# An SSD layer and a four-branch expert layer on one TensorE: the opening in another order, weight sums in pairs, one block of scores two products sooner

## The chip, the cores and the metric

One core of a Trainium2 chip runs the whole program in one launch. The core has TensorE (PE, matrix products; its weight loads are shown apart as PEld), VectorE (DVE), ScalarE (ACT), GpSimd (POOL) and SyncE (SP, which here issues almost all transfers). The metric is the device time of one launch in microseconds, as the median of several runs; lower is better. A separate execution is recorded by the profiler; the lines below come from it.

## The reference

The first part is a chunked state-space layer (32 pairs of batch and head, 768 steps, head width 32, state width 16). The second multiplies its output, 3072 tokens of 256 channels, with four experts and adds them, weighted by the normalised `domain_probs`. In brief (`la` is the logarithm of `a` in the chunk):

```python
    for c in range(nc):
        cum = np.cumsum(la, axis=-1)
        L = np.exp(cum[:, :, :, None] - cum[:, :, None, :]) * causal
        M = np.einsum('bhin,bhjn->bhij', Cc, Bc) * L
        y_intra = np.einsum('bhij,bhjd->bhid', M, xc)
        y_inter = np.einsum('bhin,bhnd->bhid', Cc, state) * np.exp(cum)[..., None]
        y[:, :, sl] = y_intra + y_inter
        state = decay_full * state + np.sum(Bx, axis=2)
...
    p = domain_probs / (domain_probs.sum(-1, keepdims=True) + 1e-09)
    for e in range(E):
        h = np.maximum(x @ w1[e], 0.0)
        out += p[:, e:e + 1] * (h @ w2[e])
```

## The kernel before

Everything is float32. The sequences are cut in chunks of 128 steps, 24 in all (4 batches by 6), numbered so that chunk `c` belongs to batch `c % 4`. A chunk holds all 8 heads, as 4 quarters of two. For each chunk the kernel makes *scores* (`score`, L502: C times B), *decays*, their product `MT` (`masked`, L681, or L856 in the plan), and from it with the values `xb` the chunk's output and its state (`inner`, L546; for later chunks also L879, which adds the state carried over). Decays of the first three chunks come from the raw `a`: `spread` (L660) copies a row to all partitions by a matmul with ones, and `scan` (L519) multiplies along it; chunks 3 to 5 scan a copy `ab` that was loaded with every row on all partitions (from `acut_d`, which the kernel writes itself); later ones use an exponential of sums of logarithms (`cum_d`).

The expert part is done as a fast matrix multiplication: 20 products instead of 24 for three pairs of chunks (a block) and four slices of weights of 256 hidden units (a unit; scheme `G`), and 7 instead of 8 for the first of them (scheme `B`). It needs sums of weights: `G.sums` lists them, `operands` makes them (L1024, one sum of 128x256 after another, on GpSimd or VectorE), stores them to `w_d` for the next block, and loads them again later. Two sums share a tile of 128x512 (`G.shared`). Four of the eight raw blocks are needed as they are (`G.raw`); where the sums are read back, these are loaded half a tile at a time (128 KB). A product is `product` (L933), two matmuls of 128x128 by 128x256, each of which shows as two records; `gated` (L968) applies the ReLU and the weight of the expert, `combine` (L960), `adjust` (L1071), `snap` (L942) and `seed` (L947) form the sums on the other side, `outputs` copies the output of a chunk (L894) and its state (L556).

Two ways of ordering the work stand beside each other. The opening, down to the first product, is written out by hand: loads on SyncE, preparation on GpSimd and VectorE (`clip`, L608; `pc`, L619, the normalised probabilities), then `spread`, `score`, `scan_quarters`, `aside` (ScalarE copies a score tile out of PSUM, L675, and GpSimd multiplies it, L676), `masked` (VectorE multiplies out of PSUM, L681), `fade` (L540, the part of the state), `turn_gates` (L646, a transpose and its copy `p_sb`, L647), `spread_gate` (L652) and `inner`. `idle` (L684) issues matmuls whose result nobody reads. The rest goes through a planner (`Plan`): each piece of work has a duration per engine, values it reads and writes, and the planner fixes the order of every engine's instructions by simulated times, from a start `now` and a time at which each engine is free (`plan.run`). The order in TensorE's line is given (`line`); `PAIRS_AT` says at which product of which unit the scores (`s`) and the outputs (`o`) of a pair of chunks stand. Each engine's queue is fixed in the program: an instruction that waits holds up what stands behind it, on SyncE and ScalarE also transfers.

Of the kernel before, what the change touches and what calls it, by code (L numbers as in the profile page):

```python
# [31 lines left out]
URGENT = {}  # L32
# [6 lines left out]
HORIZON, OPENING, LOADED = 26.0, 80.0, 1.0  # L39
ORDERS = (0, 1, 2, 3), (3, 1, 2, 0), (0, 1, 2, 3), (3, 1, 2, 0)  # L40
PAIRS_AT = ((1, 24, "s0"), (2, 1, "o0"), (2, 1, "s1"), (2, 24, "s2"), (3, 1, "o12")), (
# [28 lines left out]
class Plan:  # L70
# [109 lines left out]
    def run(self, line, at, begin):  # L180
# [17 lines left out]
        self.stall, self.port, self.bus = [], 0.0, begin["SP"] + 4  # L198
# [103 lines left out]
class Scheme:  # L302
# [9 lines left out]
G.sums = ((15, 13, 10, -1), (9, 11, 10, -1), (0, "a", 16, -1), (2, "c", 11, -1), (1, "c", 13, -1),  # L312
          (14, 16, 13, -1), (3, "e", 10, -1), (7, 10, "c", -1), (18, "d", 10, -1), (17, "d", 16, -1),
          (8, 16, 11, -1), (19, "a", 13, -1), (6, "a", 11, -1), (12, 13, "d", -1), (5, "e", 16, -1),
          (4, 11, "e", -1))
# [6 lines left out]
G.shared = {1: ((15, 9), (0, 2), (1, 14), (3, 7), (18, 17), (8, 19), (5, 6), (12, 4)),  # L322
            2: ((9, 15), (7, 2), (19, 3), (17, 12), (14, 4), (8, 5), (18, 1), (6, 0))}
# [36 lines left out]
def kernel(  # L360
# [60 lines left out]
    def some(n, shape, name, pool=const):  # L421
# [19 lines left out]
        "dram": [None],  # L441
# [137 lines left out]
    nc.sync.dma_start(out=xb[0][:, OBT:], in_=xbc[real(0)][:, OBT:])  # L579
    nc.sync.dma_start(  # L580
        out=a_sb, in_=a.rearrange("c h s -> (c h) s").rearrange("(p r) s -> p r s", r=2))
    nc.sync.dma_start(out=xb[1][:, OBT:], in_=xbc[real(1)][:, OBT:])
# [4 lines left out]
    load_tokens(2, xb[2])  # L587

# [18 lines left out]
    def clip(engine, v, top=1.0):  # L607
# [11 lines left out]
    nc.gpsimd.tensor_mul(  # L619
        pc.rearrange("p (k q) e -> p q k e", q=NSEQ), pr.rearrange("p (q k) e -> p q k e", q=NSEQ),  # L620
        total_p.rearrange("p (q k) e -> p q k e", q=NSEQ).to_broadcast([P, NSEQ, NC, E]))
# [5 lines left out]
    nc.gpsimd.memset(a_cut[:, :, 0:1], 0.0)  # L627

# [3 lines left out]

    store_decays(nc.sync, acut_d, a_cut)
    load_tokens(3, xb[3])
    for fb in range(2, 4):
        load_w1(fb, homes["W"][fb])
    for fb in range(4):
        load_w2(fb, homes["W"][4 + fb])
    load_decays(3, homes["ab"][0])
# [31 lines left out]
    gs = [homes["W"][-1][:, NT * P * i:NT * P * (i + 1)].rearrange("p (t s) -> p t s", t=NT) for i in range(2)]  # L671
# [21 lines left out]
    idle(BANK[7], 3)  # L693
    spread(0, four)
    idle(BANK[6], 3)
    mask(0, ctm[0], xb[0])
    score([0], ctm[:1], xb[:1], seven)
    scan_quarters(0, LT[0], four, 0)
    aside(0, 0, seven[0])
    aside(0, 1, seven[1])  # L700
# [288 lines left out]
    def operands(k, scheme, fbs, l, loaded={}, keep=True):  # L989
# [8 lines left out]
        def view(r):  # L998
            return views[r]()
# [564 lines left out]
```

## Time and profile before

| | us |
|---|---|
| median of 3 runs | 612.3 (612.06 to 612.62) |
| the profiled execution, whole | 612.72 |
| its span, first to last instruction | 610.94 |
| first product (L933) begins | 12.61 |
| last copy of a result on ScalarE ends | 607.73 |
| TensorE busy in the span | 603.7 |

The profile has a page (busy time of each engine, 40 slices, the chain of work that ended last, groups of instructions) and can be asked for more: a timeline, tables by stage, waits. A line of the timeline has the start, the length, the engine, the line of the kernel, the operation, out and in with partitions and elements, how many instructions are merged in it, and in square brackets the idle time before it and what ended it. The page's 40 slices of 15.3 us give the busy share of each engine in tenths; GpSimd works in the first half of the span only:

```profile
DVE  7899997988879894887969988396785989575775
ACT  5267365487642327868352334734444142434441
POOL 6565546556461001676400100200000000000000
```

### The profile page before, as it was taken

What the parts mean: (1) busy time and instruction counts of PE and PEld (TensorE: products, weight loads), DVE (VectorE), ACT (ScalarE), POOL (GpSimd) and SP (SyncE); (2) the same over time, 40 slices, a digit from 0 to 9 for tenths busy, and PEclk for the clock granted to TensorE, in tenths of its full rate; (3) what the DMA queues carried; (4) which work ended last, traced back from release to release, by engine and by line L of the source; (5) the groups of instructions that cost most, each with busy time, mean ns of one, the idle gap of its engine ahead of it and who ended that gap; (6) DMA issues with size and microseconds to landing.
All of it is one profiled execution on the core that took longest, in us unless ns stands there. A gap on an engine that the chain in (4) does not pass through costs nothing.

```text
span 610.9 us, 10142 instructions
## 1 busy us (share of the span) xinstructions
PE 603.7 (99%) x3365; PEld 513.6 (84%) x3365; DVE 489.8 (80%) x854; ACT 292.9 (48%) x681; POOL 158.8 (26%) x238
## 2 busy tenths in 40 slices
PE   9999999999999999999999999999999999999997
PEld 5778778888888888888888888888888888888885
DVE  7899997988879894887969988396785989575775
ACT  5267365487642327868352334734444142434441
POOL 6565546556461001676400100200000000000000
PEclk9999999999999999999999999999999999999999
DMA  7757668566853429893332425863142232953001
GB/s 253 257 185 222 194 215 326 187 213 228 285 160 98 113 36 328 280 313 124 134 117 87 149 47 140 274 237 118 55 127 80 87 91 63 341 187 121 1 0 53
DMA packets 89060, 99.65 MB, mean 163 GB/s; under 512 B 27428, under 2 KB 58928, under 8 KB 89008
## 3 DMA queue, kind: packets, MB, share of 16 engines
q1 hardware_dynamic: 88852, 98.95, 51.3%
q8 instruction: 27, 0.44, 0.3%
q14 instruction: 25, 0.20, 0.1%
q10 hardware_dynamic: 156, 0.06, 0.0%
HBM read 78.80 MB, written 20.17 MB: 162 GB/s over the span
## 4 chain that ended last, share of the span: by engine, by line
PE 92%; DVE 2%; ACT 1%; issue 0%; DVEq 0%
PE bank L933 88%; PE bank L546 2%; PE bank L502 1%; PE bank L879 1%; ACT A L556 1%; DVE v L968 1%; DVE v L960 0%; DVE MT L856 0%; ACT v L894 0%; DVE bank L1071 0%; DVE v L1260 0%; PE bank L1325 0%; DVE v L1425 0%; ACT LT L894 0%; ACT v L1330 0%
## 5 line engine op out<-in xcount | busy, mean ns | idle before, releaser
L933 PE MATMUL bank<-v,w 128*128 128x256 f32 x1676 | 394.8, 380 | 0.8 <-DVE bank L1071 0.7
L933 PEld LDWEIGHTS bank<-v,w 128*128 128x128 f32 x1676 | 316.9, 190 | 48.2 <-issue 2.2
L933 PE MATMUL bank<-Y,w 128*128 128x256 f32 x692 | 177.6, 381 | 0.7 <-ACT LT L894 0.4
L1213 ACT COPY v<-bank 128x512 f32<-128x512 f32 x109 | 64.0, 587 | 178.5 <-PE bank L933 166.2
L933 PEld LDWEIGHTS bank<-Y,w 128*128 128x128 f32 x692 | 130.2, 190 | 22.4 <-issue 2.0
L968 DVE SCALAR_TENSOR_TENSOR v<-bank,gate 128x512 f32<-128x512 f32 x149 | 102.3, 688 | 42.6 <-PE bank L933 39.7
L960 DVE TENSOR_TENSOR v<-v,v 128x512 f32<-128x512 f32 x181 | 126.6, 719 | 1.7 <-ACT v L942 0.3
L1071 DVE TENSOR_TENSOR bank<-bank,v 128x512 f32<-128x512 f32 x84 | 57.4, 696 | 35.7 <-PE bank L933 23.4
L942 ACT COPY v<-bank 128x512 f32<-128x512 f32 x100 | 58.6, 587 | 54.0 <-PE bank L933 45.0
L1024 POOL TENSOR_TENSOR w<-w,w 128x256 f32<-128x256 f32 x94 | 73.1, 794 | 42.5 <-DVE v L960 14.5
L947 ACT COPY bank<-v 128x512 f32<-128x512 f32 x127 | 74.0, 595 | 10.7 <-DVE v L968 8.7
L933 PE MATMUL bank<-LT,w 128*128 128x256 f32 x208 | 52.7, 379 | 0.0
L526 ACT ACTIVATE MT<-ab,neg 128x128 f32<-128x128 f32 x144 | 47.1, 396 | 2.1 <-DMA ab<-cum_d 2.1
L933 PEld LDWEIGHTS bank<-LT,w 128*128 128x128 f32 x208 | 39.4, 190 | 5.3
L531 POOL TENSOR_SCALAR_AFFINE_SELECT MT<-MT 128x512 f32<-128x512 f32 x36 | 23.2, 655 | 69.2 <-ACT MT L526 53.9
L1024 POOL TENSOR_TENSOR w<-w 128x256 f32<-128x256 f32 x32 | 24.3, 763 | 18.8 <-DVE Y L1043 7.7
L960 DVE TENSOR_TENSOR v<-bank,v 128x512 f32<-128x512 f32 x26 | 17.9, 688 | 11.1 <-PE bank L933 9.9
L856 DVE TENSOR_TENSOR MT<-bank,MT 128x512 f32<-128x512 f32 x36 | 22.7, 681 | 0.1
L1260 DVE TENSOR_TENSOR v<-v,v 128x256 f32<-128x256 f32 x55 | 21.1, 422 | 1.0 <-ACT v L1213 0.7
L960 POOL TENSOR_TENSOR v<-v,v 128x512 f32<-128x512 f32 x6 | 7.7, 1277 | 49.7 <-DVE v L960 49.7
L968 DVE SCALAR_TENSOR_TENSOR v<-v,gate 128x512 f32<-128x512 f32 x26 | 19.8, 763 | 0.4
L495 ACT ACTIVATE ctm<-xb,tmask 128x128 f32<-128x128 f32 x48 | 15.8, 395 | 3.8 <-DMA xb<-in_xbc_dram 3.7
(110 smaller groups left out, 315.1 us busy)
## 6 DMA issues: line engine op xcount, KB each, us to landing
w<-w_d SPq DMA_DIRECT2D x128, 256.0 KB
w_d<-w SPq DMA_DIRECT2D x64, 256.0 KB
w<-in_w_dram SPq DMA_DIRECT2D x40, 256.0 KB
ab<-cum_d SPq DMA_DIRECT2D x18, 512.0 KB
w<-in_w_dram SPq DMA_DIRECT2D x64, 128.0 KB
gate<-p_d SPq DMA_DIRECT2D x15, 384.0 KB
xb<-in_xbc_dram SPq DMA_DIRECT2D x17, 192.0 KB
out_dram<-v SPq DMA_DIRECT2D x144, 16.0 KB
```

Of the source, the lines that this page charges most:

```text
L526: nc.scalar.activation(out=MT[:, place(c, h), 0:P], in_=ab[:, h * P:h * P + P], func=AF.Exp, bias=neg[:, h % NT, NQ * real(c) + h // NT:NQ ...
L531: nc.gpsimd.affine_select(out=MT[:, h:h + n, 0:P], in_=MT[:, h:h + n, 0:P], compare_op=ALU.is_ge, fill=0.0, base=0, pattern=[[0, n], [1, P ...
L856: nc.vector.tensor_mul(to, g, LT0[:, js, h] if cs[0] < SCANNED else to)
L933: nc.tensor.matmul(out=o, lhsT=w[:, j], rhs=x if half is None else x[:, j], start=(start and j == 0), stop=(j == 1), skip_group_check=True)
L942: act(.5, lambda e: nc.scalar.copy(out=flat(v), in_=bank.t), reads=[bank], writes=[v])
L947: act(.54 if to - lo > FB else .32, lambda e: nc.scalar.copy(out=bank.t[:, lo:to], in_=flat(v)[:, lo:to]), reads=[v], writes=[bank])
L960: plan.add(engines, lambda e: (on(e).tensor_add if sign > 0 else on(e).tensor_sub)(flat(v), whole(x), whole(y)), reads=[x, y], writes=[v], ...
L968: dve(D512, lambda e: nc.vector.scalar_tensor_tensor(out=h.t, in0=whole(x).rearrange("p (j m) -> p j m", j=JJ), scalar=0.0, in1=g.t[:, 2 * ...
L1024: plan.add(B256, lambda e, r=r, x=x, y=y, sign=sign: (on(e).tensor_add if sign > 0 else on(e).tensor_sub)(view(r), view(x), view(y)), two= ...
L1071: dve(D512, lambda e: (nc.vector.tensor_add if sign > 0 else nc.vector.tensor_sub)(to.t, bank.t, whole(x)), reads=[x, bank], writes=[to])
L1213: act(.5, lambda e: nc.scalar.copy(out=flat(v), in_=bank.t), reads=[bank], writes=[v], hold=HOLD)
L1260: plan.add(engines, lambda e: (on(e).tensor_add if sign > 0 else on(e).tensor_sub)(o[1](), x[1](), y[1]()), reads=[v for v in vs if v is n ...
```

## The change

The opening's loads: tokens of chunk 1 are issued before `a`; chunk 3's tokens and the third and fourth slice of w1 follow at once; the store of `a_cut` moves from SyncE to ScalarE's queue; chunk 3's `ab` is loaded before the four slices of w2, not after. `pc` is computed after `a` is clipped. The third `idle` goes, and the second has two tiles, not three. Both chunks' C are masked ahead of the scores. Of chunk 0, all four score tiles go by `aside` (two went by `masked`); of chunk 1, all four by `masked` (one went by `aside`). Chunk 1's spread and scans come before that; the gate's spread comes before chunk 0's output, and chunk 2's spread, which the planner placed, stands by hand before chunk 1's output. The logarithm, its sums and the stores of `cum_d` and `p_d` go to the planner, whose start, free times and some durations change. `G.sums` names pairs of sums made by one instruction of 128x512 (7 pairs and 2 single sums, where there were 16), `G.shared` pairs them so, and raw blocks are loaded in pairs as one transfer of 256 KB (`load_pair`). The scores of the second block's first pair stand at product 22 of the unit, not 24.

```diff
-HORIZON, OPENING, LOADED = 26.0, 80.0, 1.0
+HORIZON, OPENING, LOADED = 26.0, 80.0, -1.0
-PAIRS_AT = ((1, 24, "s0"), (2, 1, "o0"), (2, 1, "s1"), (2, 24, "s2"), (3, 1, "o12")), (
+PAIRS_AT = ((1, 22, "s0"), (2, 1, "o0"), (2, 1, "s1"), (2, 24, "s2"), (3, 1, "o12")), (
...
+G.ends = ("a", "c"), ("d", "e")
+G.sums = (((15, 9), (13, 11), 10), (0, "a", 16), ((1, 2), "c", (13, 11)), ((14, 8), 16, (13, 11)),
+          ((18, 3), ("d", "e"), 10), (7, 10, "c"), ((17, 5), ("d", "e"), 16),
+          ((19, 6), "a", (13, 11)), ((12, 4), (13, 11), ("d", "e")))
...
+G.shared = {1: ((15, 9), (0, 7), (1, 2), (14, 8), (18, 3), (17, 5), (19, 6), (12, 4)),
+            2: ((15, 9), (0, 7), (1, 2), (19, 6), (18, 3), (17, 5), (12, 4), (14, 8))}
...
     nc.sync.dma_start(out=xb[0][:, OBT:], in_=xbc[real(0)][:, OBT:])
+    nc.sync.dma_start(out=xb[1][:, OBT:], in_=xbc[real(1)][:, OBT:])
     nc.sync.dma_start(
         out=a_sb, in_=a.rearrange("c h s -> (c h) s").rearrange("(p r) s -> p r s", r=2))
-    nc.sync.dma_start(out=xb[1][:, OBT:], in_=xbc[real(1)][:, OBT:])
...
     load_tokens(2, xb[2])
+    load_tokens(3, xb[3])
+    for fb in range(2, 4):
+        load_w1(fb, homes["W"][fb])
...
-    store_decays(nc.sync, acut_d, a_cut)
-    load_tokens(3, xb[3])
-    for fb in range(2, 4):
-        load_w1(fb, homes["W"][fb])
-    for fb in range(4):
-        load_w2(fb, homes["W"][4 + fb])
-    load_decays(3, homes["ab"][0])
...
     idle(BANK[6])
-    idle(BANK[7], 3)
+    idle(BANK[7], 2)
     spread(0, four)
-    idle(BANK[6], 3)
     mask(0, ctm[0], xb[0])
+    mask(1, ctm[1], xb[1])
     score([0], ctm[:1], xb[:1], seven)
     scan_quarters(0, LT[0], four, 0)
     aside(0, 0, seven[0])
     aside(0, 1, seven[1])
+    store_decays(nc.scalar, acut_d, a_cut)
     scan_quarters(0, LT[0], four, 1)
-    fade(0, MT[0], xb[0], LT[0])
-    mask(1, ctm[1], xb[1])
     spread(1, four)
     for r in (2, 3):
-        masked(0, r, MT[0], LT[0], seven[r], 0)
-    turn_gates(BANK[7])
-    nc.scalar.activation(out=a_sb, in_=a_sb, func=AF.Ln)
-    next_ = [BANK[4], BANK[0], BANK[1], BANK[6]]
+        aside(0, r, seven[r])
+    fade(0, MT[0], xb[0], LT[0])
+    turn_gates(seven[0])
+    load_decays(3, homes["ab"][0])
+    for fb in range(4):
+        load_w2(fb, homes["W"][4 + fb])
+    score([1], ctm[1:], xb[1:2], seven)
     scan_quarters(1, LT[1], four, 0)
-    score([1], ctm[1:], xb[1:2], next_)
-    aside(1, 0, next_[0])
-    y = BANK[7][:, :NT * (P + N)].rearrange("p (t s) -> p t s", t=NT)
+    spread_gate(four[0], homes["gate"][0])
+    y = four[1][:, :NT * (P + N)].rearrange("p (t s) -> p t s", t=NT)
     for t in range(NT):
         inner(0, t, y[:, t], xb[0], MT[0], P + N, t == 0)
...
-    spread_gate(BANK[5], homes["gate"][0])
-    for r in (3, 1, 2):
-        masked(1, r, MT[1], LT[1], next_[r], 0)
...
-    store_decays(nc.sync, cum_d, sums)
+    for r in (3, 0, 1, 2):
+        masked(1, r, MT[1], LT[1], seven[r], 0)
+    third = [seven[0], seven[3], four[2], four[3]]
+    spread(2, third)
...
-    nc.sync.dma_start(out=p_d.rearrange("e c s -> c e s"), in_=p_sb)
...
-    now = 13.2
+    now = 12.0
...
-    def source(fb, l, i):
+    def load_pair(v, fbs, l, f, i):
 
-        e, f = divmod(fb, EPB)
+        e, fb = divmod(fbs[f], EPB)
         if l == 1:
-            return w1[e, i * P:i * P + P, f * FB:f * FB + FB]
-        return w2[e, f * FB:f * FB + FB, i * P:i * P + P].rearrange("(j p) m -> p j m", p=P)
+            nc.sync.dma_start(out=v.t, in_=w1[e, i * P:i * P + P, fb * FB:fb * FB + 2 * FB])
+        else:
+            nc.sync.dma_start(
+                out=v.t.rearrange("p (j m) -> p j m", m=P),
+                in_=w2[e, fb * FB:fb * FB + 2 * FB, i * P:i * P + P].rearrange("(j p) m -> p j m", p=P))
...
+        def both(r):
+            if r in where and isinstance(r, tuple):
+                return where[r].t.rearrange("p (a j f) -> p a j f", a=2, j=JJ)
+            return view(r).unsqueeze(1).to_broadcast([P, 2, JJ, P])
...
+            for pair in (*scheme.raw, *(() if keys[0] in w_d else scheme.ends)):
+                v = value("W")
+                paired(v, pair)
+                f, i = scheme.blocks[l][pair[0]]
+                dma(lambda e, v=v, f=f, i=i: load_pair(v, fbs, l, f, i), part=[v])
...
+            for r, x, y in scheme.sums:
+                if isinstance(r, tuple):
+                    plan.add(B512, lambda e, r=r, x=x, y=y: difference(e, both(r), both(x), both(y)),
+                             two=True, reads=[where[x], where[y]], part=[where[r]], lean=True)
...
+    act(.3, lambda e: nc.scalar.activation(out=a_sb, in_=a_sb, func=AF.Ln), writes=[logs])
+    for r in range(2):
+        dve(.35, lambda e, r=r: sum_logs(e, r), reads=[logs], part=[cum])
+    dma(lambda e: store_decays(nc.sync, cum_d, cum.t), kb=96, reads=[cum], writes=[cd])
+    dma(lambda e: nc.sync.dma_start(out=p_d.rearrange("e c s -> c e s"), in_=p_sb), kb=48, writes=[pd])
...
-    done = plan.run(line, now, {"PE": now, "DVE": now - .2, "ACT": now + 1.0, "POOL": now - 2.0,
+    done = plan.run(line, now, {"PE": now, "DVE": now - .8, "ACT": now + 1.1, "POOL": now - 1.2,
                                 "SP": now + LOADED})
```

## The prediction

> **What bounds the kernel now.** I read the share of busy time first, then the chain of work that ended last, then a table of stages, then the opening's timeline, and last the weight-load rows with an idle time before them. The page:
>
> ```profile
> PE 603.7 (99%) x3365; PEld 513.6 (84%) x3365; DVE 489.8 (80%) x854; ACT 292.9 (48%) x681; POOL 158.8 (26%) x238
> ...
> PE 92%; DVE 2%; ACT 1%; issue 0%; DVEq 0%
> ```
>
> TensorE is the bound: 92% of the chain. The stages that I cut (start:end, length, then each engine's busy time, clock, DMA share, GB/s) show how tight:
>
> ```profile
> 3.74:12.60 8.86, 8.51 (x84) 4.81 (x83) 7.92 (x19) 4.92 (x17) 5.13 (x10) 1.00 0.95 303
> 12.60:24.30 11.70, 11.70 (x70) 9.96 (x66) 9.12 (x15) 4.08 (x14) 7.80 (x13) 1.00 0.84 284
> 24.30:56.00 31.70, 31.51 (x214) 23.70 (x213) 30.22 (x50) 19.59 (x53) 17.38 (x26) 1.00 0.64 204
> 56.00:125.00 69.00, 67.75 (x466) 56.52 (x465) 61.75 (x110) 37.65 (x110) 38.84 (x58) 1.00 0.70 231
> ...
> 235.00:601.00 366.00, 366.00 (x1900) 318.35 (x1899) 280.11 (x469) 169.23 (x357) 49.90 (x67) 1.00 0.45 141
> ```
>
> From 235 us on TensorE never rests, and no product is added or taken out, so nothing can be won there. What can move is the start of the first product (L933 at 12.60) and the waits between it and 125 us, where VectorE is 95% busy (30.22 of 31.70) and then 89%. The opening, from the timeline (start, length, engine, line, what ended the idle time):
>
> ```profile
> 4.67 1.07 POOL L608 TENSOR_SCALAR cum<-cum 96x256 f32<-96x256 f32 x1
> ...
> 4.68 2.43 DVE L519 TENSOR_TENSOR_SCAN LT<-bank,ident 128x256 f32<-128x256 f32 x4 [0.17 <-PE bank L660]
> ...
> 6.62 1.42 POOL L676 TENSOR_TENSOR MT<-w,LT 128x256 f32<-128x256 f32 x2 [0.27 <-ACT w L675]
> ...
> 7.03 0.73 DVE L681 TENSOR_TENSOR MT<-bank,LT 128x256 f32<-128x256 f32 x2
> ...
> 7.68 2.42 DVE L519 TENSOR_TENSOR_SCAN LT<-bank,ident 128x256 f32<-128x256 f32 x4
> ...
> 10.82 1.21 PE L546 MATMUL bank<-MT,xb 128*32 128x144 f32 x16
> ...
> 11.96 0.71 PE L660 MATMUL bank<-v,const-float32-1.0 32*128 32x256 f32 x8
> ...
> 12.61 3.72 PE L933 MATMUL bank<-v,w 128*128 128x256 f32 x16
> ...
> 13.55 2.43 DVE L519 TENSOR_TENSOR_SCAN LT<-bank,ident 128x256 f32<-128x256 f32 x4
> ```
>
> VectorE sets the pace: two masked products (7.03) stand between the scans of chunks 0 and 1, and chunk 2's scans wait until 13.55. The waits that follow (weight-load rows):
>
> ```profile
> 25.19 0.89 PEld L546 LDWEIGHTS bank<-MT,xb 128*32 128x32 f32 x30 [0.40 <-DVE MT L856]
> ...
> 43.22 2.46 PEld L933 LDWEIGHTS bank<-Y,w 128*128 128x128 f32 x12 [0.41 <-ACT v L942]
> ...
> 47.20 0.73 PEld L933 LDWEIGHTS bank<-v,w 128*128 128x128 f32 x4 [0.47 <-DVE v L968]
> ...
> 72.94 2.46 PEld L933 LDWEIGHTS bank<-v,w 128*128 128x128 f32 x12 [1.06 <-POOL w L1024]
> ...
> 82.47 0.73 PEld L933 LDWEIGHTS bank<-Y,w 128*128 128x128 f32 x4 [0.84 <-ACT LT L894]
> ...
> 123.35 0.73 PEld L933 LDWEIGHTS bank<-Y,w 128*128 128x128 f32 x4 [0.53 <-ACT v L894]
> ```
>
> About 0.23 of such an idle time is there at every change of work. Products follow each other 0.216 us a record; beyond that I count 0.45 lost at 24-26 us, 1.3 in seven small waits from 31 to 48, 0.85 at 72 (the row names GpSimd, but VectorE's L1071 ended only at 72.82), 0.44 at 82, 0.3 at 123 and again near 232: 3.6 us in all.
>
> **The opening, step by step.** SyncE now issues tokens of chunk 1 (0.43 us) ahead of `a`, so `a` is issued at 2.8, not 2.35; the clip started 2.32 after its issue (4.67), so now at 5.1. GpSimd then runs clip, copy, memset (starts 1.14, 0.45 and 0.1 apart: to 6.8), `pc` (moved behind them, 0.4) and four masked products where there were two before the fade, 0.68 apart: 7.2, 7.9, 8.6, 9.3. Chunk 0's fade ends near 10.4 (8.41 before), chunk 1's at 10.7.
>
> ScalarE masks chunk 1 early, copies two score tiles (0.37 each, to 6.5), issues the store of `a_cut` once GpSimd's memset is done (6.9), and copies two more by 7.9. Those wait behind the store, and GpSimd needs the third at 8.6: covered by 0.9 us. On SyncE that store took 0.34; ScalarE's two issues in this trace took 0.40 and 1.19, so at worst the cover is just used up.
>
> VectorE loses the two masked products, so chunk 1's scans run 7.05 to 9.43 instead of 7.68 to 10.10, and chunk 1's masked products, now four (0.34 apart, the first 0.1 after the scan), end at 10.96, against 11.29.
>
> TensorE is as before up to chunk 1's scores (8.43, behind the 0.26 us copy of `p_sb`; 0.67 to the next). Then the gate's spread (1.1), and chunk 0's output product, free at 10.2 but waiting for the fade: 10.4. Then spread of chunk 2 at 11.03 (0.63 later, as 9.10 to 9.73), chunk 1's output at 11.67 (0.64, as 11.96 to 12.60), done 0.70 later at 12.37; ScalarE's copy (0.27) now stands bare, where chunk 2's spread covered it: first product at **12.7**, 0.1 later than before. Bounds: without the wait for GpSimd 12.5; with `a` 0.8 later still (1.19 on SyncE, and its turn behind the next load) 13.5. I take 12.7, since every term has a row. The filler matmuls taken out (0.91 at 4.59) let chunk 0's scores start 0.35 earlier, which buys nothing: the scans, not the scores, are next in line.
>
> **After the first product.** Chunk 2's spread now precedes the wait for chunk 1, so its scans start at 11.8 instead of 13.55. `ab` of chunk 3 is loaded behind the early store, ahead of the four w2 loads: its scan started at 19.22 because the DMA came then, and now waits for VectorE at about 15.9 (two sums of logs, 0.35 each, and one gate, 0.65, come first). Adding 2.34 for that scan, 0.65 for each gate and 0.6 for each of the four L856 products, these end at 22.5, against 25.14. TensorE asks for them at 12.1 after its first product, 24.8. So the 0.45 goes; bounds 0 to 0.5. The four w2 loads queue behind that wait on SyncE and land some 1.5 us later (512 KB at about 350 GB/s); the first is used 8.4 us after the first product, at 21, and landed near 14: covered.
>
> ScalarE's logarithm (0.42) and SyncE's stores of `p_d` and `cum_d` move behind the first product; the heads' decays that read `cum_d` were loaded by 22.3 and serve L879 at 33.89, so 4 us later is covered.
>
> VectorE is then 2.3 to 2.6 us ahead. Of the 1.3 us at 31-48, the waits on L968 are answers of a queue that is full and those on L942 are ScalarE's copies, which the lead doesn't shorten; bounds 0 to 1.3, I take half, 0.65.
>
> Sums two at a time: 144 of 256 columns become 32, and 56 of 512. GpSimd: 126 by 0.77 to 0.79 (97.4 us) become 30 by 0.79 and 50 by 1.28 (87.5). VectorE: 18 by 0.42 become 2 by 0.42 and 6 by 0.72, 2.4 us less, and with four fewer L960 (0.72) 5.3 less. This lies beside TensorE; it counts only as slack at 24-125 us. A paired sum reads one operand twice; no row shows that form on GpSimd, the nearest (L968, broadcast gate, VectorE) takes 0.69, less than a plain 0.72, so I price it as plain; if it took double (2.55), 64 us would be added over 200 us of an engine that is 50 to 60% busy there, and the sums would come late by some us: it widens the upper end by 1. The 64 raw loads of 128 KB become 32 of 256 KB: SyncE saves about 32 by 0.45, for which nobody waits, as DMA is 64 to 70% busy there.
>
> Scores two products sooner: after them stood two products (1.73 us), and the third waited 0.85 for L1071, queued behind a L856 and a L968. Now four products (3.47) stand there, and the adjustment follows two L856: about 3.1 after the scores' start, against a need at 4.6. I take 0.7 of the 0.85; bounds -0.3 (the scores themselves find a bank not free) to 0.85. The waits on L894 (82, 123, 232) come from ScalarE's copies, which are not touched: 0.
>
> **Sum.** +0.1 - 0.45 - 0.65 - 0.7 = -1.7. The profiled execution took 612.72 (span 610.94 and 1.78 around it), 0.4 over the median of 612.3; so 611.0 for it, and **610.6** for the median.
>
> **Rivals.**
> (1) The opening gets earlier too, which the change's constants claim (the plan's start goes from 13.2 to 12.0). For it: VectorE and the tail of chunk 1 are earlier. Against: scores at 8.43 and five TensorE steps behind them. It would need about 1.2 off, 609.4.
> (2) The lead buys nothing: small waits are latencies from TensorE through ScalarE and back, and at 72 GpSimd's sum (the name in the row) takes L1071's place. For it: L942 and L894 names, and GpSimd's half-full queue; against: VectorE at 95%. Only the 0.45 is won, 0.1 lost: 612.0.
> (3) Slower: the warm-up. The first four filler records took 3.18 us for 1,792 columns (1.77 ns each), the products 3.72 for 4,096 (0.91): TensorE starts at about half rate. Fillers are cut from 2,560 column passes to 1,536, so TensorE rests from about 3.5 to 3.95 and 4.7 to 5.05. If the full rate then comes only after chunk 1's scores, the steps from 8.43 (0.67, 1.1, 0.63, 0.64, 0.70: 3.7 us) double: 610.6 + 3.7 = 614.3. It decides from 8.4 us on; each half-rate product record adds 0.216. Against: the granted clock was 1.00 in every stage, and the work that remains from 3.95 to 8.4 is the same.
>
> The Trainium skill ("TensorE: Matmul & The Clock Gate", Part 1) says that the array starts at half its clock and is let up only after about 3.4 us of sustained work, seen through a window that runs free of the kernel. The two rates above agree with it; how much rest such a window forgives no run here shows.
>
> **How the numbers follow.** About what a measurement of this kernel can tell from no change is 0.2%, 1.2 us. Forecast 0.46, its own range 609.7 to 611.7 (0.38 faster, 0.08 same); (1) 0.15, faster; (2) 0.19, same; (3), or a broadcast sum at double price, 0.20, slower. So faster 0.53, same 0.27, slower 0.20. The range, 608.9 to 613.6, takes in (1) and (2) and leaves out most of (3).
>
> **What would show it.** First product at 12.5 to 13.0, chunk 0's output waiting for GpSimd; scans of chunk 2 from about 11.8; no idle time on L856 near 25; the wait near 72 gone, those on L894 still there. Wrong if the first product is below 12.2 or above 13.5, if early matmuls stay at the 1.77 ns rate past 8 us, or if GpSimd's paired sums take over 1.6 us and TensorE waits for them.

## The result, and the profile after

The changed kernel is slower: 614.75 us (median, 614.41 to 614.9) against 612.52 for the kernel before, measured beside it (612.06 to 613.17). The ratio is 1.0036, its 95% interval 1.0024 to 1.0048. The profiled execution took 614.75, with a span of 612.8 us (612.72 and 610.94 before).

The page of the changed kernel: busy time by engine, the clock granted to TensorE in 40 slices, and the chain that ended last.

```profile
PE 604.5 (99%) x3363; PEld 514.9 (84%) x3363; DVE 491.5 (80%) x838; ACT 292.1 (48%) x682; POOL 157.9 (26%) x198
...
PEclk7999999999999999999999999999999999999999
...
PE 96%; ACT 1%; DVE 1%; issue 0%; DMA 0%; POOL 0%; SPq 0%; ACTq 0%; POOLq 0%
```

TensorE still sets the end, and only the first slice of the clock is not full. The table of stages of the same kernel shows that slice (start:end, length, busy time of PE, PEld, DVE, ACT, POOL, granted clock, DMA share, GB/s):

```profile
3.74:7.30 3.56, 3.01 (x23) 1.87 (x24) 3.42 (x8) 2.17 (x7) 1.60 (x4) 1.00 0.86 266
7.30:14.10 6.80, 6.45 (x43) 3.60 (x42) 3.43 (x8) 1.95 (x6) 6.05 (x11) 0.50 0.69 216
```

The same two stages of the kernel before have a clock of 1.00 and 1.00. The clock records behind the table are sharper: full from 3.88 us, half from 7.29, full again from 14.12. What that does, in the opening's timeline:

```profile
5.01 0.71 PE L502 MATMUL bank<-ctm,xb 32*128 32x256 f32 x8 [0.47 <-ACT ctm L495]
...
7.54 2.77 POOL L672 TENSOR_TENSOR MT<-w,LT 128x256 f32<-128x256 f32 x4
...
8.77 1.24 PE L502 MATMUL bank<-ctm,xb 32*128 32x256 f32 x8 [0.35 <-ACT p_sb L642]
...
9.94 2.08 PE L647 MATMUL bank<-p_sb,ident 96*128 96x128 f32 x8
...
11.95 1.19 PE L546 MATMUL bank<-MT,xb 128*32 128x144 f32 x16
...
13.06 1.21 PE L655 MATMUL bank<-v,const-float32-1.0 32*128 32x256 f32 x8
...
14.20 0.70 PE L546 MATMUL bank<-MT,xb 128*32 128x144 f32 x16
...
15.24 0.70 ACT L556 COPY A<-bank 64x16 f32<-64x16 f32 x4
...
15.99 1.35 PE L932 MATMUL bank<-v,w 128*128 128x256 f32 x5 [1.09 <-ACT A L556]
```

The same eight score matmuls take 0.71 at 5.01 and 1.24 at 8.77; the gate's spread takes 2.08 where the kernel before needs 1.16, chunk 0's output 1.19 instead of 0.70, chunk 2's spread 1.21 instead of 0.71. Together 0.53 + 0.92 + 0.49 + 0.50 = 2.4 us. Then the first product waits for something that the prediction hadn't: not for ScalarE's copy of chunk 1's output, but for the four copies of the states (L556, 0.70) behind it. It starts at 15.99 instead of 12.61: 3.4 us late. From there to the end of the span it takes 596.8 us, against 598.3: 1.5 us are won back. The waits in that part, from the weight-load rows:

```profile
27.99 0.89 PEld L546 LDWEIGHTS bank<-MT,xb 128*32 128x32 f32 x32 [0.33 <-issue]
...
46.29 2.46 PEld L932 LDWEIGHTS bank<-Y,w 128*128 128x128 f32 x12 [0.41 <-ACT v L941]
49.36 1.59 PEld L932 LDWEIGHTS bank<-v,w 128*128 128x128 f32 x8 [0.62 <-DVE v L967]
...
71.37 0.73 PEld L932 LDWEIGHTS bank<-Y,w 128*128 128x128 f32 x4 [0.33 <-ACT v L1232]
...
84.34 0.73 PEld L932 LDWEIGHTS bank<-Y,w 128*128 128x128 f32 x4 [0.83 <-ACT v L893]
...
125.21 0.73 PEld L932 LDWEIGHTS bank<-Y,w 128*128 128x128 f32 x4 [0.51 <-ACT v L893]
```

The wait of chunks 2 and 3 near 25 us is down to what any change of work costs, that of 1.06 at 72 us is gone (0.33 behind the scores is again a change of work). Those at 46 to 49 and those on ScalarE's copies stand as before.

### The profile page after: what moved, and what is told of

The parts are those of the page before. It is cut to its first block, busy times and chain, and to the rows that moved or that the text cites. A ratio compares the mean times of both kernels' runs of the same rounds, so it can differ in the third digit from the quotient of the medians.

```text
span 612.8 us, 9986 instructions
## 1 busy us (share of the span) xinstructions
PE 604.5 (99%) x3363; PEld 514.9 (84%) x3363; DVE 491.5 (80%) x838; ACT 292.1 (48%) x682; POOL 157.9 (26%) x198
## 4 chain that ended last, share of the span: by engine, by line
PE 96%; ACT 1%; DVE 1%; issue 0%; DMA 0%; POOL 0%; SPq 0%; ACTq 0%; POOLq 0%
PE bank L932 91%; PE bank L502 2%; PE bank L546 2%; PE bank L878 1%; ACT A L556 1%; PE bank L655 1%; DMA xb<-in_xbc_dram 0%; ACT v L893 0%; PE bank L647 0%; DVE v L967 0%; DVE v L1279 0%; PE bank L1344 0%; ACT ctm L495 0%; DVE Y L1062 0%; DVE v L959 0%
## 5 line engine op out<-in xcount | busy, mean ns | idle before, releaser
L1232 ACT COPY v<-bank 128x512 f32<-128x512 f32 x106 | 62.1, 585 | 180.8 <-PE bank L932 170.9
L967 DVE SCALAR_TENSOR_TENSOR v<-bank,gate 128x512 f32<-128x512 f32 x148 | 101.6, 687 | 43.6 <-PE bank L932 40.4
L959 DVE TENSOR_TENSOR v<-v,v 128x512 f32<-128x512 f32 x174 | 124.0, 732 | 1.1 <-ACT v L941 0.2
L992 POOL TENSOR_TENSOR w<-w,w 128x512 f32<-128x512 f32 (+1 forms) x76 | 84.8, 1128 | 51.6 <-DVE v L959 16.6
L1090 DVE TENSOR_TENSOR bank<-bank,v 128x512 f32<-128x512 f32 x81 | 55.3, 696 | 36.6 <-PE bank L932 23.8
L941 ACT COPY v<-bank 128x512 f32<-128x512 f32 x101 | 58.9, 586 | 47.2 <-PE bank L932 39.5
L932 PE MATMUL bank<-LT,w 128*128 128x256 f32 x216 | 55.3, 379 | 0.0
L932 PEld LDWEIGHTS bank<-LT,w 128*128 128x128 f32 x216 | 41.0, 190 | 5.6
L967 DVE SCALAR_TENSOR_TENSOR v<-v,gate 128x512 f32<-128x512 f32 x26 | 19.8, 762 | 0.4
L959 DVE TENSOR_TENSOR v<-v,LT 128x512 f32<-128x512 f32 x21 | 17.8, 849 | 0.1
L1232 ACT COPY LT<-bank 128x512 f32<-128x512 f32 x15 | 8.8, 585 | 18.9 <-PE bank L932 18.9
```

Source lines behind the costliest of these rows:

```text
L932: nc.tensor.matmul(out=o, lhsT=w[:, j], rhs=x if half is None else x[:, j], start=(start and j == 0), stop=(j == 1), skip_group_check=True)
L941: act(.5, lambda e: nc.scalar.copy(out=flat(v), in_=bank.t), reads=[bank], writes=[v])
L959: plan.add(engines, lambda e: (on(e).tensor_add if sign > 0 else on(e).tensor_sub)(flat(v), whole(x), whole(y)), reads=[x, y], writes=[v], ...
L967: dve(D512, lambda e: nc.vector.scalar_tensor_tensor(out=h.t, in0=whole(x).rearrange("p (j m) -> p j m", j=JJ), scalar=0.0, in1=g.t[:, 2 * ...
L992: (on(e).tensor_add if sign > 0 else on(e).tensor_sub)(out, x, y)
L1090: dve(D512, lambda e: (nc.vector.tensor_add if sign > 0 else nc.vector.tensor_sub)(to.t, bank.t, whole(x)), reads=[x, bank], writes=[to])
```

## The experiments

Each was timed beside the kernel before, whose median was 612.50 to 612.72 in these comparisons. *First* is the start of the first product, *rest* the span less that, both of one profiled execution, in us; *half* counts the executions whose mean granted clock was 0.994 or less, which is what 6.8 us at half clock make of it (0.5 x 6.83 of 612.8).

| run | median (range) | ratio, 95% | first | rest | half |
|---|---|---|---|---|---|
| before | 612.52 | | 12.61 | 598.3 | none |
| after | 614.75 (614.41 to 614.9) | 1.0024 to 1.0048 | 15.99 | 596.8 | 4 of 7 |
| e1_fill | 613.95 (612.32 to 614.96) | 1.0011 to 1.0028 | 14.29 | 596.6 | 0 of 11 |
| e2_more | 613.63 (612.73 to 614.45) | 1.0008 to 1.0026 | 15.16 | 596.9 | 0 of 11 |
| e3_bank | 614.13 (613.49 to 614.91) | 1.0015 to 1.0033 | 15.19 | 596.6 | 9 of 11 |
| e4_both | 613.73 (612.88 to 614.75) | 1.0011 to 1.0028 | 13.98 | 597.1 | 0 of 11 |
| f1_cut | 614.22 (613.37 to 615.69) | 1.0017 to 1.0035 | 14.56 | 597.4 | 7 of 10 |
| f2_lead | 612.12 (612.01 to 612.95) | 0.9986 to 1.0003 | 13.27 | 597.3 | 0 of 11 |
| f3_pairs | 614.42 (614.09 to 615.49) | 1.0016 to 1.0037 | 13.28 | 599.4 | 0 of 8 |
| f4_both | 613.77 (613.11 to 614.68) | 1.0010 to 1.0028 | 12.60 | 599.5 | 0 of 11 |
| g2_bank | 613.54 (611.73 to 614.73) | 1.0003 to 1.0021 | 12.82 | 597.1 | 0 of 11 |
| g1_dve | 613.55 (611.95 to 614.84) | 1.0007 to 1.0025 | 12.64 | 598.9 | 0 of 11 |
| g3_plain | 613.31 (612.27 to 613.71) | 1.0000 to 1.0018 | 12.82 | 598.9 | 0 of 11 |
| g4_cand | 612.71 (612.3 to 614.21) | 0.9996 to 1.0014 | 13.17 | 599.2 | 0 of 11 |
| h1_w2 | 616.97 (616.2 to 617.8) | 1.0056 to 1.0083 | 18.64 | 597.4 | 4 of 5 |
| h2_logs | 616.87 (616.5 to 617.24) | 1.0057 to 1.0082 | 18.22 | 597.1 | 4 of 5 |
| h3_plain | 616.38 (615.54 to 617.07) | 1.0048 to 1.0073 | 16.94 | 597.5 | 3 of 5 |
| h4_plainlogs | 616.75 (616.34 to 617.05) | 1.0053 to 1.0079 | 17.88 | 597.1 | 5 of 5 |
| i1_store | 613.6 (612.35 to 614.17) | 1.0007 to 1.0025 | 13.16 | 597.7 | 0 of 11 |
| i3_plainlogs | 613.69 (613.19 to 613.9) | 1.0009 to 1.0027 | 13.17 | 598.3 | 0 of 11 |

A profile shows one execution, and with *first* depending on when the clock is granted it needn't be the median one: g2_bank's was the fastest of its eleven, g4_cand's the slowest. So the verdicts go by the medians, and the profiles say where.

A part of some times lies behind the last instruction. The time less the span is 1.67 to 1.83 us in every execution of the kernel before, but up to 2.84 in g1_dve, 2.75 in e1_fill and 2.92 in f4_both. It goes with a line of the page's section on DMA queues (queue and kind: packets, MB, share), here of g1_dve and of g4_cand:

```profile
q8 instruction: 26, 0.43, 0.3%
...
q8 instruction: 27, 0.44, 0.3%
```

Eight kernels have 26 packets there: the changed kernel, e1_fill, f3_pairs, f4_both, g1_dve, g2_bank, h1_w2 and i1_store. They alone have a time less span of more than 1.84. In the profiles of e1_fill, f3_pairs and g1_dve a transfer of 16 KB on this queue ends 2.4 to 3.1 us behind the span, as the last thing on record. All eight have paired sums, but so do four kernels with 27 packets. By the medians of the spans alone g1_dve is 0.8 above the kernel before and 0.6 above g4_cand, not 1.0 and 0.84.

### Fillers and a bank, in the changed kernel

**e1_fill**

```diff
-    idle(BANK[7], 2)
+    idle(BANK[7], 3)
     spread(0, four)
+    idle(BANK[6], 3)
```

> The changed kernel with the filler matmuls of before put back (four, three and three tiles instead of four and two). Theory C (the clock: too few fillers, so that TensorE's granted clock falls to half from 7.3 to 14.1 us of the opening, which lengthens five steps by 2.4 us): the half-clock stretch is gone or much shorter, the first product starts at about 13.6 instead of 15.99, and the time falls from 614.75 to about 612.4. Rival O (the new order itself: GpSimd's four masked products and the loads behind ScalarE's store set the opening): the clock may change, but the first product stays at 15.5 or later and the time within 0.5 us of 614.75. A third possibility, C2: the new order rests TensorE in other places, so that the same fillers are not enough: the half-clock stretch stays at 5 us or more and the time at 614 or above.

The opening's timeline of this run:

```profile
5.04 0.91 PE L680 MATMUL bank<-const-float32-1.0 128*128 128x384 f32 x2
...
9.02 0.71 PE L502 MATMUL bank<-ctm,xb 32*128 32x256 f32 x8 [0.47 <-ACT p_sb L642]
...
14.29 3.72 PE L933 MATMUL bank<-v,w 128*128 128x256 f32 x16 [1.10 <-ACT A L556]
```

The scores of chunk 1 are back at 0.71, the first product is 1.7 earlier, and no execution's mean clock shows the 6.8 us at half clock (one, 0.997, has about half as much). A late first grant would not show in that mean, as f1_cut below tells. The clock part of theory C holds in the profile; the time fell by 0.80, a third of what it asked for, and executions now spread over 2.6 us.

**e2_more**: e1_fill, and

```diff
     score([0], ctm[:1], xb[:1], seven)
+    for _ in range(3):
+        idle(BANK[6][:, FB:], 2)
...
     turn_gates(seven[0])
+    idle(BANK[1][:, FB:], 1)
...
     spread_gate(four[0], homes["gate"][0])
+    idle(BANK[7][:, FB:], 2)
```

> As the run before, and more filler matmuls wherever TensorE rests in the opening: three of two tiles behind chunk 0's scores, one tile behind the turning of the gates, two tiles behind the gate's spread. Theory C: the granted clock stays full from about 3.8 us on, the first product starts at 13.3 to 13.8, the time is 612.0 to 612.6, whatever run e1_fill does. Rival O: full clock, and still a first product at 15.5 or later, the time within 0.5 us of 614.75.

613.63, 0.32 under e1_fill, which the spread doesn't separate. A filler that runs before the clock is granted stands in TensorE's queue at half rate: here the fillers at 5.26 took 1.29 and chunk 0's scores began at 6.48 (5.01 in the changed kernel). More fillers than before's weren't needed to hold the clock: e1_fill's profile kept it as well.

**e3_bank**

```diff
     for c in range(2):
         st[c]["A"] = plan.taken("A", c, now)
+    for b in (four[0], seven[1]):
+        plan.homes["bank"][homes["bank"].index(b)].free = now + .7
```

> The changed kernel with the two banks that chunk 1's output products fill told to the planner as free 0.7 us later, so that the first product takes another bank and no longer waits for ScalarE's copies of the states. Theory B (0.7 us of the late first product is that wait on the bank): the first product starts at about 15.3 instead of 15.99, with ScalarE's copies of yT as what it waits for, and the time falls by 0.5 to 0.8, to about 614.1; the half-clock stretch stays. Rival: the wait is ScalarE's copies of yT or a weight that lands late, and the first product stays within 0.2 us of 15.99.

```profile
15.19 3.07 PE L934 MATMUL bank<-v,w 128*128 128x256 f32 x13
```

As expected in size: 0.8 earlier and 0.62 off the time, with no idle time left to show on TensorE. Only banks changed; the order of every engine's instructions is that of the changed kernel. Half clock stays (9 of 11). **e4_both** is e2_more with this edit:

> The fillers of e2_more and the free bank of e3_bank together in the changed kernel. Theories C and B together: first product at 12.6 to 13.1, body as in the changed kernel (596.8 us from there to the end), so 611.0 to 611.8, which is 0.8 to 1.5 us below the kernel before. Rival O: above 613.5.

613.73: a miss. The first product came at 13.98, not 12.6 to 13.1. In this profile the full clock came at 5.56, fillers at half rate held chunk 0's scores until 6.25, and from there TensorE's rows show no idle time. GpSimd's fade ended at 10.9, 1 us before chunk 0's output (11.88), so GpSimd wasn't the hold-up here: the fillers themselves were in the way. More fillers and the bank together don't bring the time back.

### Parts of the change in the old opening

**f1_cut**, the kernel before with

```diff
-    idle(BANK[7], 3)
+    idle(BANK[7], 2)
     spread(0, four)
-    idle(BANK[6], 3)
```

> The kernel before with nothing changed but the filler matmuls, cut from four, three and three tiles to four and two as in the changed kernel. Theory C (fewer fillers cost TensorE its clock in the opening, in any order): full clock comes later or is lost again by some windows of 3.4 us in most executions, and the time rises from 612.5 by 0.8 to 2.4, to 613.3 to 614.9. Rival C2 (the new order rests TensorE, not the number of fillers): the time stays within 0.3 us of 612.5 and the record shows full clock from about 3.8 us on.

A stage of this run (columns as above), and then its opening's timeline:

```profile
7.30:13.18 5.88, 5.88 (x38) 3.67 (x36) 5.19 (x13) 1.64 (x6) 2.59 (x6) 1.00 0.95 307
```

```profile
3.80 1.24 PE L660 MATMUL bank<-v,const-float32-1.0 32*128 32x256 f32 x8
...
9.04 1.24 PE L502 MATMUL bank<-ctm,xb 32*128 32x256 f32 x8
...
14.56 2.64 PE L932 MATMUL bank<-v,w 128*128 128x256 f32 x11
```

Theory C, in the middle of its range: four filler tiles cost 1.56 us with nothing else changed. This execution was never granted the full clock before 13.18 us. The column of the clock says 1.00 all the same, and its mean is 0.999: it counts only what is on record, and until the first grant nothing is. The durations tell (1.24 for what takes 0.71). So an execution of the changed kernel with a mean of 1.00, as three of seven had, needn't have had the full clock in the opening; they took 614.41 to 614.78, on average 0.3 less than the other four. One thing more: *rest* is 597.4, 0.9 shorter than before's 598.3, though nothing in it was touched. TensorE begins late, the others catch up, and the wait near 25 us is gone here too:

```profile
26.56 0.89 PEld L546 LDWEIGHTS bank<-MT,xb 128*32 128x32 f32 x32 [0.33 <-POOL cts L839]
```

**f2_lead**, the kernel before with

```diff
-PAIRS_AT = ((1, 24, "s0"), ...
+PAIRS_AT = ((1, 22, "s0"), ...
```

> The kernel before with nothing changed but the place of the scores at 69 to 72 us, two products sooner (24 becomes 22). If what I read in the trace holds (0.7 of the 0.85 us wait on the adjusted bank near 72 us goes), 611.8, within 0.3; the wait is gone from the weight-load rows. Rival: the wait moves to the next product or the scores wait for a bank, and the time stays within 0.2 us of 612.5.

612.12 against 612.66: 0.54 less, with an interval that just includes no change. In its trace the scores come at 67.69 and the next product 0.33 behind their end; the wait at 72 is gone. The lowest median of the study.

```profile
67.69 0.74 PEld L502 LDWEIGHTS bank<-ctm,xb 32*128 32x128 f32 x16 [0.33 <-DMA w_d<-w]
68.76 0.73 PEld L933 LDWEIGHTS bank<-Y,w 128*128 128x128 f32 x4 [0.33 <-POOL cts L840]
```

**f3_pairs**, the kernel before with the new `G.raw`, `G.ends`, `G.sums`, `G.shared` and `operands`; **f4_both**, that with f2_lead's edit.

> The kernel before with nothing changed but the sums of weights: two at a time where the pairs allow it, and raw weights loaded in 32 loads of 256 KB. Theory: these lie beside TensorE, within 0.3 us of 612.5, with GpSimd's paired sums at about 1.28 us each. Rival P (paired sums are the loss: a late sum makes TensorE wait): 613 or more, with weight-load rows that name GpSimd.

> The opening of before with the paired sums and the scores two products sooner: what is left of the change when its opening is taken out. Theory: the loss of the changed kernel is its opening alone and the rest wins 0.7 (the wait at 72) plus whatever paired sums give: 611.3 to 612.0, so faster than the kernel before by 0.5 to 1.2. Rival P: 612.5 or more.

Rival P: f3_pairs is 1.76 us slower than the kernel before, and f4_both 1.65 slower than f2_lead. Both carry the loads of 256 KB with the paired sums; no run separates the two. Groups of instructions first (line, shapes, count, then busy time and mean ns of one, then idle time ahead of them), of f3_pairs:

```profile
L993 POOL TENSOR_TENSOR w<-w,w 128x512 f32<-128x512 f32 x52 | 67.8, 1311 | 34.0 <-DVE v L960 12.3 <-PE bank L933 6.2 <-issue 5.0
...
L1063 DVE TENSOR_TENSOR Y<-Y,Y 128x256 f32<-128x256 f32 x12 | 8.7, 726 | 0.4 <-PE bank L933 0.4
```

and the same twelve sums of tokens in the kernel before:

```profile
L1043 DVE TENSOR_TENSOR Y<-Y,Y 128x256 f32<-128x256 f32 x12 | 5.3, 438 | 0.4 <-PE bank L933 0.4
```

A paired sum costs GpSimd 1.31 on average, nearly as a plain operation of its size (1.28, six of L960 on GpSimd in the kernel before). But some of VectorE's operations with both operands in SBUF became longer: 438 to 726 ns for these twelve, though only 719 to 735 for the many of L960. The timeline of f3_pairs shows one case to its end:

```profile
50.40 1.27 POOL L993 TENSOR_TENSOR w<-w,w 128x512 f32<-128x512 f32 x1 [0.69 <-DVE v L960]
50.78 1.44 DVE L960 TENSOR_TENSOR v<-v,v 128x512 f32<-128x512 f32 x1
...
52.15 0.69 DVE L1091 TENSOR_TENSOR bank<-bank,v 128x512 f32<-128x512 f32 x1
52.37 1.27 POOL L993 TENSOR_TENSOR w<-w,w 128x512 f32<-128x512 f32 x1 [0.69 <-DVE v L960]
...
52.98 1.10 PE L933 MATMUL bank<-Y,w 128*128 128x256 f32 x4 [1.01 <-DVE bank L1091]
```

GpSimd starts a paired sum at 50.40, VectorE's L960 starts inside it and takes 1.44 instead of 0.68, ending 0.55 after the sum; the adjustment behind it (L1091) is late, and TensorE stands 1.01 us. The Trainium skill ("SBUF — State Buffer", Who interferes with whom) says that a VectorE instruction with two operands in SBUF and a GpSimd instruction that reads SBUF exclude each other for a whole instruction; these rows agree, as L960 ends late and L1091, which reads one operand from a bank, keeps its 0.69 beside the next sum.

### What is left when fillers and bank are mended

**g2_bank** is the changed kernel with e1_fill's and e3_bank's edits. **g1_dve** adds

```diff
     for r in (2, 3):
-        aside(0, r, seven[r])
+        masked(0, r, MT[0], LT[0], seven[r], 0)
```

**g3_plain** is g2_bank with before's sums and loads of weights, **g4_cand** has all of it.

> The changed kernel with before's fillers (four, three and three tiles) and the free bank for the first product, nothing more. The bank gave 0.62 us without the fillers (614.75 to 614.13) and the fillers 0.80 (to 613.95). Theory B+C (the two add up): 613.2 to 613.5, first product about 0.7 us earlier than 14.29 at the same phase of the clock, no stretch of 6.8 us at half clock in the executions. Rival (they hide each other): 613.8 or more.

> As g2_bank, and the third and fourth masked product of chunk 0 back on VectorE, between the scans of chunk 0 and chunk 1, as in the kernel before; GpSimd keeps two. Theory O2 (what is left of the opening's loss is GpSimd's chain of four products and a fade, 0.69 us each, that chunk 0's output waits for): the output product of chunk 0 no longer waits for GpSimd, the first product starts 0.3 to 0.8 us earlier than in g2_bank, and the time falls to 612.5 to 613.0. Rival (VectorE's two products push chunk 1's scans back by 0.7 us and cost the same): within 0.25 us of g2_bank.

> As g2_bank, but with the sums of weights one at a time and the raw loads of 128 KB, as in the kernel before. The paired sums cost 1.8 us in the old opening (614.42 against 612.66). Theory P (paired sums hold the port that GpSimd and VectorE share for 1.28 us at a time and cost in any plan): 612.3 to 613.0, some 0.5 us or more below g2_bank. Rival P2 (the loss in the old opening was an accident of that plan, since the changed kernel's own trace shows no such wait): within 0.3 us of g2_bank.

> All four together: before's fillers, the free bank, chunk 0's last two masked products on VectorE, and sums one at a time; of the change there remain the order of the opening, the loads and the scores two products sooner. If theories O2 and P both hold 611.7 to 612.4, below the kernel before; if only one does 612.5 to 613.0; if neither, as g2_bank.

The first product is now as early as before the change, 12.64 to 13.17, and the median is still 1 us above the kernel before in the first two. g1_dve against g2_bank: no difference (613.55, 613.54), though the output of chunk 0 no longer waits for GpSimd. g3_plain against g2_bank: 0.23 less, inside what these spreads can't tell. g4_cand comes to 612.71, not told apart from the kernel before (0.9996 to 1.0014); it differs from g1_dve by the paired sums (0.84) and from g3_plain by the two products on GpSimd (0.60), but the same two edits gave 0.23 and nothing in the other two pairs. So with four parts undone the loss of 2.2 us is gone; how much of it belongs to which depends on what else is in.

Where g1_dve loses what its early start should bring:

```profile
25.19 0.89 PEld L546 LDWEIGHTS bank<-MT,xb 128*32 128x32 f32 x30 [0.42 <-DVE MT L858]
...
34.38 0.87 PE L881 MATMUL bank<-cts,S 32*32 32x256 f32 x16 [0.41 <-POOL cts L842]
...
40.14 7.75 PE L935 MATMUL bank<-Y,w 128*128 128x256 f32 x32 [0.95 <-DVE Y L1065]
```

The wait near 25 us is back at its old size and place, and two new ones follow. The one near 25 goes with the two products that VectorE has again: in g2_bank, where GpSimd keeps them and the first product is nearly as early (12.82), VectorE's products for chunk 3 end at 24.05 and TensorE asks for them later:

```profile
24.82 0.89 PEld L546 LDWEIGHTS bank<-MT,xb 128*32 128x32 f32 x32 [0.33 <-issue]
```

The other two are not the paired sums' alone: g4_cand's profile, without such sums, has waits of 0.97 and 0.94 us at 35.05 and 40.39 in the same two places. In g1_dve SyncE stood 5.5 us at the load of `ab` that waits for ScalarE's store, and ScalarE waited 2.10 us for the heads' decays at 30.4. That made a theory: SyncE's queue.

**h1_w2** (g1_dve with the four w2 loads ahead of that load), with **h2_logs** (the logarithms, their sums and the store of `cum_d` back in the opening), **h3_plain** and **h4_plainlogs** (the two without paired sums):

```diff
-    load_decays(3, homes["ab"][0])
     for fb in range(4):
         load_w2(fb, homes["W"][4 + fb])
+    load_decays(3, homes["ab"][0])
```

> As g1_dve (613.55), and the four w2 loads are issued ahead of the load of ab that waits 5.5 us for ScalarE's store, instead of behind it. Theory S (SyncE's queue: what stands behind that wait comes late to the products at 31 to 40 us): SyncE issues the w2 loads from about 7.5 us instead of 13.3, the second ab is issued some 2 us earlier, the waits at 31 to 40 us shrink by half or more, the time falls by 0.5 to 1.0, to 612.5 to 613.0. Rival (those waits come from the later store of cum_d alone, or from VectorE): within 0.25 us of 613.55.

> As h1_w2, and the logarithm, the two sums of logs and the store of cum_d back in the opening as in the kernel before, where the heads' decays were loaded at 19.5 us instead of 24.6. Theory S2 (the late heads' decays make the products at 33 us wait): no wait for GpSimd's cts there, 0.3 to 0.8 us less than h1_w2. Rival: the two sums (0.35 us each) push chunk 2's scans back and nothing is won, within 0.25 us of h1_w2.

> As h1_w2 without the paired sums (so g4_cand, 612.71, with the w2 loads ahead of the wait). Theory S: 612.0 to 612.4. Rival (the paired sums, not the queue, make the waits): as g4_cand, 612.5 to 612.9.

> As h2_logs without the paired sums: of the change there remain the order of chunk 0's and chunk 1's products, the store on ScalarE and the scores two products sooner. If theories S and S2 hold, 611.3 to 612.0, the best of all; if neither, 612.5 to 612.9.

616.97, 616.87, 616.38 and 616.75: all wrong, by 4 us. From the timeline of h1_w2:

```profile
11.36 0.35 ACTq L633 DMA_DIRECT2D acut_d<-v  x1
...
11.75 0.26 ACT L642 COPY p_sb<-bank 96x128 f32<-96x128 f32 x1 [3.71 <-POOL v L1232]
12.07 0.51 PEld L502 LDWEIGHTS bank<-ctm,xb 32*128 32x128 f32 x8 [3.48 <-ACT p_sb L642]
```

The store of `a_cut` was issued at 11.36; in g1_dve at 7.49. The trace says why: of the eight semaphores that these transfers use in turn, the store now has the one of the load of chunk 2's tokens (issued 5.38, landed 11.29) and waits for it; in g1_dve it has one whose transfer had landed at 6.21. ScalarE stands in line behind it, the copy of the gates too, TensorE rests 3.3 us and the clock goes: half from 9.84 to 20.08. In the other three the store stands at 10.60 to 11.44. It says nothing on the queue. Behind so late a start the *rest* is 597.1 to 597.5 with paired sums and without.

**i1_store** takes the store off ScalarE, in the order store, w2, `ab`; **i3_plainlogs** adds before's sums of weights and h2_logs' edit.

```diff
-    store_decays(nc.scalar, acut_d, a_cut)
+    store_decays(nc.sync, acut_d, a_cut)
```

> As g1_dve (613.55) with the store of a_cut issued by SyncE again, then the four w2 loads, then the load of ab that waits for the store. ScalarE waits for no transfer. Theory S (SyncE standing 5.5 us at that load, with the w2 loads, the second ab and the heads' decays behind it): w2 loads issued by about 11 us, first product at 12.6 to 13.3, the waits at 31 to 40 us shrink by half or more, 612.5 to 613.0. Rival (those waits come from the later store of cum_d and from VectorE): within 0.25 us of 613.55.

> As i1_store, with sums of weights one at a time and the logarithm, the two sums of logs and the store of cum_d back in the opening. If the queue, the late heads' decays and the paired sums all cost what the theories say, 611.3 to 612.0, under the kernel before (612.6); if only the paired sums do, 612.5 to 612.9 as g4_cand.

i1_store: 613.6 against 613.55. The w2 loads went out from 8.28 and the wait for GpSimd's `cts` is gone, but that for Y is still there (1.23 at 39.52 in the weight-load rows, 1.33 at 40.11 in g1_dve). The rival holds: no gain from SyncE's queue shows beside the spread. i3_plainlogs, 613.69, is 1.0 above g4_cand, from which it differs by the store, the queue and the earlier sums of logs: together these lose. It is also no faster than i1_store, from which it differs by the paired sums and the sums of logs.

## Why the prediction was wrong

- **The opening, +0.1: this step failed.** It measured +3.4 in the profile. "The filler matmuls taken out ... buys nothing" is the sentence that fell: they held the clock. Cut alone they cost 1.56 us (f1_cut), put back they return 0.80 (e1_fill). The rest of the failed step is "ScalarE's copy (0.27) now stands bare": the first product's bank is one that chunk 1's output had filled, so it waits for the copies of the states as well, 0.62 (e3_bank). In the profile the two come to 2.4 and about 0.8 of the 3.4.
- **Rival 3** had the cause, the place (steps behind 8.4 us) and nearly the time, 614.3. That the time came so near is partly luck. The rival had the clock granted late, as in f1_cut's profile; here it was granted at 3.88 and lost at 7.29. The doubled steps were to cost 3.7 and cost 2.4, and the wait on the bank, which the rival didn't have, made up most of the rest. I gave it 0.20, together with broadcast sums at double price, on account of a granted clock of 1.00 in every stage. Those rows were right for the kernel before (full clock from 3.74), but they show an opening with its fillers in and say nothing of one without. f1_cut's row of 1.00 shows besides that the column reads so where nothing is on record.
- **GpSimd's chain** ran 7.54 to 10.31 for 7.2 to 10.0 forecast, and chunk 0's fade ended near 10.7 instead of 10.4; the gate's spread at half clock, not the fade, held chunk 0's output until 11.95. Sizes nearly right, and they decided nothing here.
- **The wait at 24 to 26, -0.45:** gone, and the reason given holds as far as it goes: g2_bank and g3_plain, with VectorE's whole lead and a first product at 12.82, don't have it, and g1_dve, where two products are VectorE's again, has it back. But a late start alone removes it too (f1_cut), so in the changed kernel the lead bought nothing that the delay had not already given.
- **The wait at 72, -0.7:** right in mechanism: the wait is gone. In size it is near, 0.54 by itself, but with an interval that just includes no change.
- **The small waits from 31 to 48, -0.65:** not halved; the 0.62 on L967 and the 0.41 on L941 stand.
- **The sum after the first product** came out close, -1.5 for -1.8, by offsetting errors: a late start gives something back (0.9 of 1.95 us in f1_cut), the scores 0.5.
- **Paired sums, "price as plain", beside TensorE:** right for GpSimd (1.30 for 1.28), wrong for who pays. The price is VectorE's, 1.7 us in the old order, loads of 256 KB included. In the new order it isn't settled: the four pairs of runs that differ by it alone give 0.84, 0.59, 0.23 and 0.12, and only the first looks clear of the spread. The upper end had 1 for a broadcast that costs double; the mean of 1.30 has no room for that.
- **The later loads, "covered":** not contradicted; i1_store moved them and no change of the time shows.

What stays open: with fillers and bank mended and paired sums kept (g2_bank, g1_dve) one kernel's executions spread over 3 us, about twice that of the kernel before, and no profile was taken of a slow one next to a fast one. Up to about 1 us of that spread lies behind the last instruction, where nothing in these runs says what sets it. The 1 us that g1_dve's median loses to the kernel before is put down to paired sums by g4_cand alone, and i3_plainlogs, without them and no faster than i1_store, doesn't bear it out.

## What to carry to other kernels

A filler matmul is to be judged by the clock of everything behind it, not by the wait that it fills; before cutting one, look for the first full-rate duration in the rows, since the mean clock says nothing of the time before the first grant. A part that begins late runs shorter: measure a change to it with the start held fixed, or a delay passes for a gain. Longer GpSimd operations on SBUF save instructions on GpSimd and can make VectorE's two-operand operations wait; price them there.

## What the runs showed of the hardware

- The clock changes in steps of 3.41 us, counted from a point that differs between executions: first grants at 3.74, 3.88, 4.75 and 13.18 us in four profiles, full clock for one such step and half for two in the changed kernel (3.88, 7.29, 14.12), half for three in h1_w2 (9.84 to 20.08). The Trainium skill ("TensorE: Matmul & The Clock Gate", Part 1) states a free-running window of 3,413 ns; these agree.
- A busy TensorE lost its clock, and a busy one didn't get it. In the step that ended at 7.29 us it was busy for 2.94 of 3.41 us, but with matmuls of 32 rows alone; f1_cut had no grant before 13.18, though busy for all of the 5.88 us from 7.30 on. e1_fill kept the clock through a step with less work (2.54 of 3.41 us from 8.16 on), with matmuls of 96 and 128 rows in it, so the busy share isn't the rule. In all openings that kept the clock a filler of 128 rows ran after the first spread. That it is the rows that count is my reading; no run changed them alone.
- A GpSimd sum and a VectorE operation with both operands in SBUF exclude each other: an L960 of 0.68 us, begun inside a sum of 1.27, took 1.44 and ended 0.55 behind it (f3_pairs).
- A store issued by ScalarE held all of ScalarE for 3.7 us, by a semaphore that it shares with one of SyncE's loads (h1_w2).
